# A banded attention with two MLPs on one core: low gates read last, four output banks, and tile 4 at the end of layer 1

## The chip, the core and the metric

The kernel runs on one core of one Trainium2 chip. The metric is the device time of one execution. Below, PE is TensorE (its weight loads are shown apart as PEld), DVE is VectorE, ACT is ScalarE, POOL is GpSimd, and SP is the engine that issues nearly all DMAs.

## The reference

Three stages follow each other; every sum has to come out in float32 quality.

```
attn  = softmax(q k^T / 8 + bias, causal, window 128) v      # 4 batches, 8 heads, 576 x 64
x     = attn, tokens by features                             # 2304 x 512
h     = x @ w_in  (512 x 2048);  g = max(0.01 h, h)          # layer 1
x     = g @ w_out (2048 x 512)
h     = x @ w2_in (512 x 2048);  g = h * sigmoid(1.702 h)    # layer 2
out   = g @ w2_out (2048 x 512)                              # 2304 x 512
```

## The kernel before, in words

**Numbers in two halves.** A float32 operand of a matmul is kept as a high part (what the fast matmul format holds) and a low part (the rest). A product is three matmuls: high times high, high times low, low times high. `PASS` (line 505) lists them as (weight part, gate or token part). A gate `g` is made in `split` (line 526): ACT copies the high part, then POOL subtracts it from the gate to get the low part, so the low part is ready last.

**Layer 1.** 2304 tokens stand in five tiles (`TW`: 384, 512, 512, 512 and 384 columns), the 2048 hidden features in 8 chunks of two blocks of 128. A round is one chunk and one tile: `mm1` twice (12 matmuls each, one block of hidden features), then one round later `mm2` four times (6 matmuls each, one block of 128 outputs). An evacuation on DVE adds each `mm2` result to the accumulator `y`. The table `rounds` (line 716) sets the order: chunks 0 and 1 interleaved while attention still runs, then chunk by chunk, tile 0 to 4. Two sets of weight tiles alternate: even chunks in `wA`, odd chunks in `wB`. Beside this, in the same loop, the float64 weights of both layers are converted to high and low parts on ACT, DVE and POOL, and those of layer 2 are stored to DRAM (`w7d`, `wod`).

**Layer 2** multiplies with seven products in place of eight (a Strassen scheme). The tokens form three pairs p of two blocks of 384 (pair 0: tiles 0 and 1; pair 1: tiles 2 and 3; pair 2: the rest with tile 4). `build_x` (line 576) makes seven operands of a pair from `y`: 7 copies on ACT, 11 subtractions on DVE, spread over steps. It starts with pair 0 near the end of layer 1, and pair 1 starts 16 steps later. The operands lie where layer 1's tokens were (`xblocks`), so each waits until layer 1 has read its tokens. A unit (chunk i, pair p) is the seven products `prod` (line 652) and then six `out2` (line 680), each 6 matmuls of 512 columns for 128 tokens. Chunk 0 interleaves pair 0 with the last `mm2` of layer 1; pair 1 follows. Chunks 1 to 6 run the 14 products of both pairs and then a tail of 12 `out2` (in chunk 6 six of these stand beside the next unit). Chunk 7 and all of pair 2 interleave products with the `out2` of the unit before.

**Weights of layer 2** go into 15 slots (`slots`, `old`), which are the last weight tiles of layer 1: slots 0 to 6 for the seven products, 7 to 10 and 11 to 14 for the output weights of even and odd chunks. Before, slots 0 to 6 and 7 to 10 lie in tiles of chunk 6 and of chunk 7's first layer, and the first loads are issued as soon as chunk 6 is through.

**PSUM.** Each tag has two banks. `mm2` takes "mm" and "O" in turn, `out2` only "mm". A product takes "S", "O" or "pt". The order on each engine is the order in which the code issues (a manual schedule); every engine works in that order.

Of the kernel before, what the change touches and what calls it, by code (L numbers as in the profile page):

```python
# [20 lines left out]
NTT = len(TW)  # L21
NF = DFF // 128
CB = 2
NCH = NF // CB
# [9 lines left out]
def attention_mlp_kernel(  # L34
# [16 lines left out]
    def ps(tag):  # L51
        return psum.tile([128, 512], F32, tag=tag, name=tag, bufs=2)
# [4 lines left out]
    step = [0]  # L57

    def after(d, fn):
        later.setdefault(step[0] + d, []).append(fn)  # L60
# [84 lines left out]
    pending = [0]  # L145
# [381 lines left out]
    def split(u, key, more):  # L527
# [4 lines left out]
        nc.scalar.activation(g[:, 0], u, AF.Copy)  # L532
        sub(nc.gpsimd, g[:, 1], u, g[:, 0].bitcast(F32))

    def mm2(r, e):
        _, c, t = r
        ops = [(f, a, b2) for f in range(CB) for a, b2 in PASS]
        assert all((c * CB + f, 1) in ready for f in range(CB))
        y = ps("mm" if window[0] else ("mm", "O")[e % 2])[:, 0:TW[t]]
        for m, (f, a, b2) in enumerate(ops):  # L540
            nc.tensor.matmul(  # L541
                out=y, lhsT=wt[c * CB + f][:, 2 + a, e * 128:(e + 1) * 128],
                rhs=gt[r, f][:, b2, :], start=(m == 0), stop=(m == len(ops) - 1),
            )
        acc = y1[t][:, e]

        def evac():
            if c == 0:
                nc.scalar.activation(acc, y, AF.Copy)
            else:  # L550
                nc.vector.tensor_tensor(out=acc, in0=acc, in1=y, op=ALU.add)  # L551

        after(1, evac)
# [6 lines left out]
    def xblocks(extra):  # L560
        halves = [extra[:, k].rearrange("p (a k) n -> p a k n", a=2) for k in range(2)]
        parts = xs.rearrange("p (m a k n) -> p m a k n", a=2, k=2, n=TT)
        parts = [parts[:, m] for m in range(2 * NT // TT)]
        halves = parts[0:4] + halves + parts[4:]
        for p in range(3):
            xb[p] = halves[7 * (p % 2):7 * (p % 2) + 7]

    def token_block(p, t, e):
        j = 2 * p + t
# [38 lines left out]
    def load_in(i, n):  # L608
        nc.sync.dma_start(
            out=slots[n].bitcast(F32), in_=w7d[i % NCH][:, n].rearrange("p a k -> p (a k)"))  # L610
# [68 lines left out]

    def out2(i, p, t, e):  # L680
        c = i % NCH
        y = ps("mm")
        ops = [(f, a, b2) for f in range(CB) for a, b2 in PASS]
        for m, (f, a, b2) in enumerate(ops):
            nc.tensor.matmul(  # L685
                out=y, lhsT=gt[i, p, f, t][:, b2, e * 128:(e + 1) * 128],
                rhs=out_slot(i, f, a), start=(m == 0), stop=(m == len(ops) - 1),
            )
        tile_, off = token_block(p, t, e)
        acc = y1[tile_][:, :, off:off + 128]  # L690

        def evac():
            yv = y.rearrange("p (e n) -> p e n", e=4)
            if c == 0:
                nc.scalar.activation(acc, yv, AF.Copy)
            else:
                nc.vector.tensor_tensor(out=acc, in0=acc, in1=yv, op=ALU.add)  # L697
            if c == NCH - 1:
                after(1, store)

        def store():
            for u in range(2):
                b, m = divmod((T0[tile_] + off) // 64 + u, NKB)
                t1 = b * S + 64 * ORDER[b % 2][m]

                (nc.scalar if u and i == 2 * NCH - 1 else nc.sync).dma_start(
                    out=out[t1:t1 + 64, :].rearrange("r (e n) -> r e n", e=4),
                    in_=acc[64 * u:64 * u + 64])

        after(1, evac)  # L710
# [3 lines left out]

    early = ((0,), (1,), (2,), (3, 4))
    rounds = [(0, c, t) for ts in early for c in range(2) for t in ts]
    rounds += [(0, c, t) for c in range(2, NCH) for t in range(NTT)]
    groups = []
    NR = len(rounds)

# [8 lines left out]
            groups += [(j - 1, mm2, e) for e in range(4)]  # L729
    groups.reverse()  # L730

    last1 = {c: j for j, (_, c, _) in enumerate(rounds)}
    pos1, pos2 = [-1], [-1]

# [17 lines left out]
    def layer1():  # L752
        raws[0] = 3
        q1 = wconv[4 * CB:]
        q2 = [(NF + f, 1) for f in range(CB)] + [(n, 0) for n in range(NF, 2 * NF)]
        todo, wait = [], 0
        while pos2[0] < NR - 4 or q1 or q2 or todo or pending[0]:


            while q1 or q2:  # L760
                near = q1 and slot_free(*q1[0], ahead=1)
                if len(wraw) >= (3 if near or not q2 else 2):
                    break
                todo.append(((q1 if near or not q2 else q2).pop(0), step[0]))
                load_w(*todo[-1][0])
            if todo and wait <= 0 and step[0] - todo[0][1] >= 4:
                n, p = todo[0][0]
                if n >= NF or slot_free(n, p):
                    todo.pop(0)
                    if n < NF:  # L770
                        if n not in wt:
                            alloc_w(n)
                        conv_w(n, p)
                    else:
                        (conv_out if p else conv_in)(n)
                    wait = 4
            if groups:
                run_group()
            tick()
            wait -= 1  # L780

    def layer2():
        raws[0] = 2
        xblocks(tmp([128, 2, 4, TT], F32R, "xe", 1))
        old = [wt[NF - 4 + n][:, m] for n in range(4) for m in range(4)]
        slots.extend(old[n] for n in (0, 1, 2, 3, 4, 5, 6, 8, 9, 12, 13, 10, 11, 14, 15))
        for n in USE:
            load_in(0, n)


        begun = None
        while len(groups) > 6:
            run_group()
            tick()
            if begun is None and pos2[0] >= NR - 4:
                begun = step[0]
                build_x(0, 1.6)
        assert begun is not None
        after(max(1, begun + 16 - step[0]), lambda: build_x(1, 1.3))
        prev = [run_group] * len(groups)  # L800

        def outs(i, p, t):
            return [lambda e=e: out2(i, p, t, e) for e in range(3)]

        def play(ops, at):
            for t, fn in enumerate(ops):
                for g in at.get(t, ()):
                    g()
                if fn is not None:
                    fn()  # L810
                elif prev:
                    prev.pop(0)()
                tick()

        def raw_out(n):
            return lambda: load_w(n, 1)

        def make_out(n):
            return lambda: conv_out(n)

        n0 = NF + CB
        for p in range(2):
            w = unit_ops(0, p)
            play([w[0], None, w[1], w[4], None, w[5], None, w[3], None, w[6], None, w[2], None],
                 {4: [raw_out(n0 + 1)], 1: [make_out(n0)]} if p else {6: [raw_out(n0)]})
            if not p:
                load_out(0)
            prev = outs(0, p, 1) + outs(0, p, 0)


        for i in range(1, NCH - 1):
            n0 = NF + CB * (i + 1)
            lead = [None] * (len(prev) if i == 1 else 0)
            w = [unit_ops(i, p) for p in range(2)]
            ops = lead + [w[p][n] for p, n in (
                (0, 0), (1, 0), (0, 5), (0, 4), (1, 4), (1, 5), (0, 3), (1, 3), (0, 1), (0, 6),
                (1, 6), (1, 1), (0, 2), (1, 2))]
            tail = [fn for t in (1, 0) for p in range(2) for fn in outs(i, p, t)]
            last = i == NCH - 2
            m = len(ops)  # L840
            at = {m - 10: [raw_out(n0)], m - 6: [raw_out(n0 + 1)], m: [make_out(n0)],
                  m + 5: [make_out(n0 + 1)]}
            if i == 1:
                at[1] = [make_out(NF + CB + 1)]
            play(ops + (tail[:6] if last else tail), at)
            if last:
                prev = tail[6:]


        for i, p in [(NCH - 1, 0), (NCH - 1, 1)] + [(NCH + c, 2) for c in range(NCH)]:  # L850
            w = unit_ops(i, p)
            play([w[0], w[5], w[1], w[4], None, None, w[3], None, None, w[6], w[2], None, None], {})
            if p and i < 2 * NCH - 1:
                load_out(i + 1)
            if (i, p) == (NCH - 1, 0):
                after(1, lambda: build_x(2, 1.6))
            prev = outs(i, p, 1) + outs(i, p, 0)
        for _ in range(4):
            tick()
        for fn in prev:  # L860
            fn()
            tick()
        while later:
            tick()
# [145 lines left out]
```

## Time and profile before

| | |
|---|---|
| Time, median of 3 runs | 898.65 us (898.63 to 899.36) |
| The profiled execution | 898.58 us, span 896.9 us |
| PE busy | 868.3 us, 97% of the span |
| DVE, ACT, POOL busy | 597.3, 422.4, 400.6 us |
| Mean granted clock of PE | 0.988 |

PE is busy in nearly all of the span. Attention and the first layer-1 rounds fill it to some 155 us, layer 1 to about 515 us, layer 2 the rest. Times of single instructions and groups stand in the rows below. What a stall of PE costs is read best from start to start of its matmul groups, since the end of a matmul is modelled.

### The profile page before, as it was taken

What the parts mean: (1) busy time and instruction counts of PE and PEld (TensorE: products, weight loads), DVE (VectorE), ACT (ScalarE), POOL (GpSimd) and SP (SyncE); (2) the same over time, 40 slices, a digit from 0 to 9 for tenths busy, and PEclk for the clock granted to TensorE, in tenths of its full rate; (3) what the DMA queues carried; (4) which work ended last, traced back from release to release, by engine and by line L of the source; (5) the groups of instructions that cost most, each with busy time, mean ns of one, the idle gap of its engine ahead of it and who ended that gap; (6) DMA issues with size and microseconds to landing.
All of it is one profiled execution on the core that took longest, in us unless ns stands there. A gap on an engine that the chain in (4) does not pass through costs nothing.

```text
span 896.9 us, 15695 instructions
## 1 busy us (share of the span) xinstructions
PE 868.3 (97%) x5722; PEld 759.0 (85%) x5722; DVE 597.3 (67%) x1213; ACT 422.4 (47%) x1025; POOL 400.6 (45%) x441
## 2 busy tenths in 40 slices
PE   7689999999999999999999989999999999999997
PEld 5578888889898988888898979889888988899896
DVE  5889765368799998998943753674574477323333
ACT  5887885453344433543333566245235435443331
POOL 5887544254466757565552133244144242232321
PEclk6999999999999999999999999999999999999999
DMA  9764430242244254425250144244324515956552
GB/s 219 175 168 114 102 87 13 84 141 71 71 156 146 97 176 145 162 94 189 70 188 1 48 129 144 73 137 153 117 84 153 157 67 152 304 168 208 165 177 71
DMA packets 85532, 116.04 MB, mean 129 GB/s; under 512 B 40912, under 2 KB 51152, under 8 KB 84432
## 3 DMA queue, kind: packets, MB, share of 16 engines
q1 hardware_dynamic: 82064, 113.83, 41.3%
q10 hardware_dynamic: 3392, 1.21, 0.5%
q8 instruction: 46, 0.75, 0.3%
q14 instruction: 30, 0.25, 0.1%
HBM read 87.23 MB, written 27.79 MB: 128 GB/s over the span
## 4 chain that ended last, share of the span: by engine, by line
PE 80%; DVE 8%; POOL 3%; issue 3%; DMA 3%; ACT 2%; SPq 0%; POOLq 0%; ACTq 0%; DVEq 0%
PE mm L685 21%; PE S L623 10%; PE mm L541 9%; PE pt L517 7%; PE O L541 7%; PE S L517 7%; PE pt L623 5%; PE O L623 3%; PE mm L517 2%; PE O L477 2%; PE pt L442 2%; PE S L393 2%; DVE ca L169 1%; DVE x L143 1%; DVE ca L167 1%
## 5 line engine op out<-in xcount | busy, mean ns | idle before, releaser
L143 POOL TENSOR_TENSOR g<-u,g 128x512 fp32r<-128x512 f32 (+1 forms) x86 | 112.7, 1314 | 124.2 <-ACT g L532 101.4
L175 POOL TENSOR_TENSOR ca<-ca,cb 128x512 f32<-128x512 f32 x59 | 81.5, 1381 | 114.6 <-DVE cb L173 102.6
L697 DVE TENSOR_TENSOR y<-y,mm 128x512 f32<-128x512 f32 x126 | 86.4, 685 | 53.7 <-PE mm L685 52.6
L685 PE MATMUL mm<-wB,g 128*128 128x512 f32 x432 | 118.4, 395 | 0.5 <-POOL g L143 0.5
L685 PE MATMUL mm<-wB,gm 128*128 128x512 f32 x432 | 118.4, 395 | 0.2
L143 POOL TENSOR_TENSOR g<-sn,g 128x384 fp32r<-128x384 f32 x42 | 43.4, 1039 | 132.5 <-ACT g L532 108.9
L685 PEld LDWEIGHTS mm<-wB,gm 128*128 128x128 f32 x432 | 79.4, 188 | 21.2 <-POOL gm L143 2.4
L685 PEld LDWEIGHTS mm<-wB,g 128*128 128x128 f32 x432 | 81.2, 189 | 17.4 <-POOL g L143 0.8
L623 PE MATMUL S<-x,wA 128*128 128x384 f32 x384 | 75.9, 336 | 2.3 <-ACT x L588 1.8
L649 DVE TENSOR_TENSOR sn<-sn,pt 128x384 f32<-128x384 f32 x48 | 26.6, 554 | 77.2 <-ACT sn L644 52.8
L644 ACT ACTIVATE sn<-S 128x384 f32<-128x384 f32 x72 | 35.3, 490 | 83.3 <-PE S L623 83.2
L623 PEld LDWEIGHTS S<-x,wA 128*128 128x128 f32 x384 | 67.8, 188 | 5.0 <-ACT x L588 2.1
L551 DVE TENSOR_TENSOR y<-y,mm 128x512 f32<-128x512 f32 (+1 forms) x74 | 46.2, 625 | 37.0 <-PE mm L541 36.9
L541 PE MATMUL mm<-g,wA 128*128 128x512 f32 (+1 forms) x264 | 62.9, 372 | 3.3 <-POOL g L143 2.4
L541 PE MATMUL mm<-g,wB 128*128 128x512 f32 (+1 forms) x264 | 62.2, 371 | 0.0
L143 POOL TENSOR_TENSOR gm<-sn,gm 128x384 fp32r<-128x384 f32 x30 | 32.2, 1080 | 65.4 <-ACT gm L532 51.0
L523 ACT ACTIVATE u<-S 128x512 f32<-128x512 f32 (+1 forms) x34 | 18.8, 552 | 85.4 <-PE S L517 85.4
L623 PE MATMUL pt<-x,wA 128*128 128x384 f32 x288 | 57.6, 337 | 0.5 <-DVE x L143 0.5
L541 PEld LDWEIGHTS mm<-g,wA 128*128 128x128 f32 x264 | 47.6, 188 | 10.2 <-POOL g L143 3.2
L169 DVE SCALAR_TENSOR_TENSOR ca<-raw,ca 128x512 uint32<-128x512 uint32 x62 | 55.5, 895 | 0.6
L167 DVE TENSOR_SCALAR ca<-ca 128x512 uint32<-128x512 uint32 x62 | 55.2, 891 | 0.5
L635 ACT ACTIVATE sn<-sn 128x384 f32<-128x384 f32 x72 | 37.3, 518 | 36.9 <-DVE sn L649 36.9
(131 smaller groups left out, 1878.1 us busy)
## 6 DMA issues: line engine op xcount, KB each, us to landing
wA<-w7d SPq DMA_DIRECT2D x112, 256.0 KB, 3.5
w7d<-c SPq DMA_DIRECT2D x8, 1792.0 KB, 7.0
wB<-wod SPq DMA_DIRECT2D x36, 256.0 KB, 4.0
raw<-w1i SPq DMA_DIRECT2D x16, 512.0 KB, 3.5
raw<-w1o SPq DMA_DIRECT2D x16, 512.0 KB, 3.7
raw<-w2o SPq DMA_DIRECT2D x16, 512.0 KB, 4.8
raw<-w2i SPq DMA_DIRECT2D x16, 512.0 KB, 3.5
wod<-wB SPq DMA_DIRECT2D x28, 256.0 KB, 2.8
```

The source lines that it names most:

```text
L143: e.tensor_tensor(out=out, in0=in0, in1=in1, op=ALU.subtract)
L167: lambda: nc.vector.tensor_scalar(a, a, 0x07FFFFFF, 3, op0=ALU.bitwise_and, op1=ALU.logical_shift_left),
L169: lambda: nc.vector.scalar_tensor_tensor(out=a, in0=hi32, scalar=0xC0000000, in1=a, op0=ALU.bitwise_and, op1=ALU.bitwise_or),
L175: lambda: nc.gpsimd.tensor_tensor(out=af, in0=af, in1=bf, op=ALU.add),
L517: nc.tensor.matmul(out=h, lhsT=w[:, a, k * 128:(k + 1) * 128], rhs=xt[t][:, b2, k], start=(m == 0), stop=(m == len(ops) - 1),)
L541: nc.tensor.matmul(out=y, lhsT=wt[c * CB + f][:, 2 + a, e * 128:(e + 1) * 128], rhs=gt[r, f][:, b2, :], start=(m == 0), stop=(m == len(ops ...
L551: nc.vector.tensor_tensor(out=acc, in0=acc, in1=y, op=ALU.add)
L623: nc.tensor.matmul(out=out, lhsT=w[:, 256 * a + 128 * k:256 * a + 128 * k + 128], rhs=x[:, b2, k], start=(start and m == 0), stop=(stop an ...
L635: nc.scalar.activation(u, h, AF.Gelu_apprx_sigmoid)
L644: nc.scalar.activation(st[name], st["X"], AF.Copy)
L685: nc.tensor.matmul(out=y, lhsT=gt[i, p, f, t][:, b2, e * 128:(e + 1) * 128], rhs=out_slot(i, f, a), start=(m == 0), stop=(m == len(ops) - 1),)
L697: nc.vector.tensor_tensor(out=acc, in0=acc, in1=yv, op=ALU.add)
```

## The change

There are five edits.

1. `gate_order` puts a group's matmuls on the low gate part last, in `mm2` and `out2`. In `out2` the gate block with index t comes first.
2. `out2` takes "mm" and "O" in turn for chunks 1 to 6.
3. In `rounds`, tile 4 of chunks 6 and 7 moves behind tiles 0 to 3 of both.
4. The first operand build starts one round earlier, at step 1.5 in place of 1.6. Pair 1's starts when tile 3 of chunk 7 is summed, at step 1.9 in place of 1.3. The operands of pair 1 that are built last are the ones on tile 4's memory.
5. Slots 2 to 6 and 7 to 10 lie on other weight tiles. The seven first loads no longer go out together: four go out after `mm1` of chunk 6's tile 4, two after that of chunk 7's, and one after `mm2` of chunk 6's.

```diff
+    def gate_order(fs):
+        return [(f, a, 0) for f in fs for a in range(2)] + [(f, 0, 1) for f in fs]
...
     def mm2(r, e):
-        ops = [(f, a, b2) for f in range(CB) for a, b2 in PASS]
+        ops = gate_order(range(CB))
...
+        xb[1] = [xb[1][n] for n in (0, 1, 4, 3, 5, 2, 6)]
...
     def out2(i, p, t, e):
-        y = ps("mm")
-        ops = [(f, a, b2) for f in range(CB) for a, b2 in PASS]
+        y = ps(("mm", "O")[e % 2] if 0 < i < NCH - 1 else "mm")
+        ops = gate_order((t, 1 - t))
...
-    rounds += [(0, c, t) for c in range(2, NCH) for t in range(NTT)]
+    rounds += [(0, c, t) for c in range(2, NCH - 2) for t in range(NTT)]
+    rounds += [(0, c, t) for ts in ((0, 1, 2, 3), (4,)) for c in (NCH - 2, NCH - 1) for t in ts]
...
-        while pos2[0] < NR - 4 or q1 or q2 or todo or pending[0]:
+        while pos2[0] < first or q1 or q2 or todo or pending[0]:
...
-        slots.extend(old[n] for n in (0, 1, 2, 3, 4, 5, 6, 8, 9, 12, 13, 10, 11, 14, 15))
-        for n in USE:
-            load_in(0, n)
+        slots.extend(old[n] for n in (0, 1, 2, 8, 4, 5, 9, 12, 13, 3, 6, 10, 11, 14, 15))
+        build_x(0, 1.5)
+        marks = [(0, last1[NCH - 2], (0, 1, 4, 5)), (0, last1[NCH - 1], (3, 6)),
+                 (1, last1[NCH - 2], (2,))]
...
-            if begun is None and pos2[0] >= NR - 4:
-                begun = step[0]
-                build_x(0, 1.6)
+            if not half_way and pos2[0] >= second:
+                half_way = True
+                build_x(1, 1.9)
+            while marks and (pos1, pos2)[marks[0][0]][0] >= marks[0][1]:
+                for n in marks.pop(0)[2]:
+                    load_in(0, n)
-        after(max(1, begun + 16 - step[0]), lambda: build_x(1, 1.3))
```

The first place is PE at the start of the tail of layer 2's chunk 1. The numbers tell buffers apart: `g_6167` and `gm_6185` are the two gates, and `mm` or `O` is the output bank. Before, three of its twelve output groups:

```order
L685 MATMUL mm_6226<-wB_169,gm_6185 128x512 x3
L685 MATMUL mm_6226<-wB_170,g_6167 128x512 x3
L685 MATMUL mm_6239<-wB_169,gm_6185 128x512 x3
L685 MATMUL mm_6239<-wB_170,g_6167 128x512 x3
L685 MATMUL mm_6251<-wB_169,gm_6185 128x512 x3
L685 MATMUL mm_6251<-wB_170,g_6167 128x512 x3
```

The same three groups in the changed kernel, on PE:

```order
L689 MATMUL mm_6226<-wB_170,g_6167 128x512 x2
L689 MATMUL mm_6226<-wB_169,gm_6185 128x512 x2
L689 MATMUL mm_6226<-wB_170,g_6167 128x512
L689 MATMUL mm_6226<-wB_169,gm_6185 128x512
L689 MATMUL O_6239<-wB_170,g_6167 128x512 x2
L689 MATMUL O_6239<-wB_169,gm_6185 128x512 x2
L689 MATMUL O_6239<-wB_170,g_6167 128x512
L689 MATMUL O_6239<-wB_169,gm_6185 128x512
L689 MATMUL mm_6251<-wB_170,g_6167 128x512 x2
L689 MATMUL mm_6251<-wB_169,gm_6185 128x512 x2
L689 MATMUL mm_6251<-wB_170,g_6167 128x512
L689 MATMUL mm_6251<-wB_169,gm_6185 128x512
```

The low part of `gm_6185` moves from the second matmul of the group to the sixth, and the middle one of three groups takes an "O" bank, so a bank of "mm" is used again three groups later and not two.

The second place is PE at the end of layer 1; `wA` are chunk 6's weights and `wB` chunk 7's, and L623 or L627 are products of layer 2. Before, from `mm2` of chunk 7's tile 2:

```order
L541 MATMUL mm<-g,wB 128x512 x6
L541 MATMUL O<-g,wB 128x512 x6
L541 MATMUL mm<-g,wB 128x512 x6
L541 MATMUL O<-g,wB 128x512 x6
L517 MATMUL S<-x,wB 128x384 x12
L517 MATMUL pt<-x,wB 128x384 x12
L541 MATMUL mm<-g,wB 128x512 x6
L541 MATMUL O<-g,wB 128x512 x6
L623 MATMUL S<-x,wA 128x384 x6
```

In the changed kernel, on PE, from the second half of the same `mm2`:

```order
L544 MATMUL mm<-g,wB 128x512 x6
L544 MATMUL O<-g,wB 128x512 x6
L517 MATMUL S<-x,wA 128x384 x12
L517 MATMUL pt<-x,wA 128x384 x12
L544 MATMUL mm<-g,wB 128x512 x6
L544 MATMUL O<-g,wB 128x512 x6
L544 MATMUL mm<-g,wB 128x512 x6
L544 MATMUL O<-g,wB 128x512 x6
L517 MATMUL S<-x,wB 128x384 x12
L517 MATMUL pt<-x,wB 128x384 x12
L544 MATMUL mm<-g,wA 128x384 x6
L544 MATMUL O<-g,wA 128x384 x6
```

The first product of layer 2 comes right behind these twelve rows. Between the end of chunk 7's tile 2 and that product there now stands a round more than before.

The third place is ACT in layer 2's pair 1 of chunk 0: `x<-y` is an operand copy of `build_x`, `sn<-S` reads a product's running sum, `wB<-ca` ends a weight conversion. Before:

```order
L588 ACTIVATE x<-y 128x768
L532 ACTIVATE gm<-sn 128x384
L644 ACTIVATE sn<-S 128x384
L164 ACTIVATE ca<-raw 128x512
L695 ACTIVATE y<-mm 128x4x128
L588 ACTIVATE x<-y 128x768 x2
L635 ACTIVATE sn<-sn 128x384
L644 ACTIVATE sn<-S 128x384
L588 ACTIVATE x<-y 128x768
L532 ACTIVATE gm<-sn 128x384
L695 ACTIVATE y<-mm 128x4x128 x2
L225 ACTIVATE wB<-ca 128x512
```

The same place on ACT in the changed kernel:

```order
L592 ACTIVATE x<-y 128x768
L639 ACTIVATE sn<-sn 128x384
L532 ACTIVATE gm<-sn 128x384
L648 ACTIVATE sn<-S 128x384
L164 ACTIVATE ca<-raw 128x512
L699 ACTIVATE y<-mm 128x4x128
L639 ACTIVATE sn<-sn 128x384
L648 ACTIVATE sn<-S 128x384
L532 ACTIVATE gm<-sn 128x384
L699 ACTIVATE y<-mm 128x4x128 x2
L225 ACTIVATE wB<-ca 128x512
```

Of the four copies that stood in this piece one is left at its head; the other three stand further ahead, beside pair 0.

## Rows read from the trace of the kernel before

**Rows 1.** Page, part 1: engine, busy us, share of the span, instructions.

```profile
PE 868.3 (97%) x5722; PEld 759.0 (85%) x5722; DVE 597.3 (67%) x1213; ACT 422.4 (47%) x1025; POOL 400.6 (45%) x441
```

**Rows 2.** Waits of the weight loads: us in total, times, longest.

```profile
PEld mm L685 <- POOL gm L143: 2.4, 6, 0.4
PEld S L623 <- ACT x L588: 2.1, 1, 2.1
PEld mm L685 <- DVE y L697: 1.9, 6, 0.5
```

**Rows 3.** Chain in order of time, undisturbed stretch: start us, us, what.

```profile
160.31 1.36 PE mm L541 x6
...
178.73 2.08 PE pt L517 x12
```

**Rows 4.** Timeline, tail of chunk 2: start, us, engine, what, [idle before].

```profile
590.11 1.98 POOL L143 TENSOR_TENSOR gm<-u,gm 128x384 fp32r<-128x384 f32 x2
...
590.74 1.16 PE L685 MATMUL mm<-wB,gm 128*128 128x512 f32 x3
...
591.17 0.30 PEld L685 LDWEIGHTS mm<-wB,gm 128*128 128x128 f32 x2 [0.41 <-POOL gm L143]
...
607.79 0.69 PE L623 MATMUL S<-x,wA 128*128 128x384 f32 x3
```

**Rows 5.** Timeline, pair 1 of chunk 0 in layer 2: PE, ACT and POOL.

```profile
515.06 0.53 ACT L532 ACTIVATE g<-u 128x384 fp32r<-128x384 f32 x1 [0.71 <-PE O L541]
515.73 1.44 POOL L143 TENSOR_TENSOR g<-u,g 128x384 fp32r<-128x384 f32 x1 [0.24 <-ACT g L532]
516.36 0.40 PE L685 MATMUL mm<-wB,g 128*128 128x512 f32 x1
517.22 1.43 PE L685 MATMUL mm<-wB,g 128*128 128x512 f32 x5 [0.47 <-POOL g L143]
518.49 1.22 PE L623 MATMUL O<-x,wA 128*128 128x384 f32 x6
519.56 0.65 ACT L164 ACTIVATE ca<-raw 128x512 f32<-128x512 f32 x1
521.48 0.62 PE L623 MATMUL S<-x,wA 128*128 128x384 f32 x2 [1.77 <-ACT x L588]
522.47 0.97 PE L623 MATMUL S<-x,wA 128*128 128x384 f32 x4 [0.38 <-DVE x L143]
523.28 2.59 PE L685 MATMUL mm<-wB,g 128*128 128x512 f32 x6
525.67 1.77 PE L623 MATMUL pt<-x,wA 128*128 128x384 f32 x6
527.29 1.55 PE L685 MATMUL mm<-wB,g 128*128 128x512 f32 x6
...
530.37 0.63 ACT L225 ACTIVATE wB<-ca 128x512 fp32r<-128x512 f32 x1 [0.89 <-POOL ca L175]
530.42 0.85 PE L685 MATMUL mm<-wB,gm 128*128 128x512 f32 x3
531.43 0.79 PE L623 MATMUL S<-x,wA 128*128 128x384 f32 x3 [0.16 <-ACT sn L644]
```

**Rows 6.** Page, part 5: line, engine, what, count | busy us, mean ns | idle before.

```profile
L175 POOL TENSOR_TENSOR ca<-ca,cb 128x512 f32<-128x512 f32 x59 | 81.5, 1381 | 114.6 <-DVE cb L173 102.6
...
L169 DVE SCALAR_TENSOR_TENSOR ca<-raw,ca 128x512 uint32<-128x512 uint32 x62 | 55.5, 895 | 0.6
L167 DVE TENSOR_SCALAR ca<-ca 128x512 uint32<-128x512 uint32 x62 | 55.2, 891 | 0.5
```

**Rows 7.** Windows: stretch; us; PE, PEld, DVE, ACT, POOL busy; PEclk; DMA; GB/s.

```profile
500.00:516.00 16.00, 16.00 (x88) 15.27 (x87) 14.10 (x19) 10.23 (x17) 3.04 (x4) 1.00 0.07 23
523.30:526.50 3.20, 3.20 (x10) 2.65 (x9) 3.17 (x5) 1.76 (x4) 0.00 (x0) 0.53 0.59 203
```

**Rows 8.** Loads of the product slots (line 609), issue to landing.

```profile
DMA to landing us min/median/max: 2.5/3.5/7.2
```

More of the change, by code (lines that the diff above doesn't have):

```diff
@@ L730, in attention_mlp_kernel @@
     groups.reverse()
+    first, second = (rounds.index((0, NCH - 1, t)) for t in (1, 3))
     last1 = {c: j for j, (_, c, _) in enumerate(rounds)}
@@ L785, in layer2 @@
         old = [wt[NF - 4 + n][:, m] for n in range(4) for m in range(4)]
-        slots.extend(old[n] for n in (0, 1, 2, 3, 4, 5, 6, 8, 9, 12, 13, 10, 11, 14, 15))
-        for n in USE:
-            load_in(0, n)
-        begun = None
+        slots.extend(old[n] for n in (0, 1, 2, 8, 4, 5, 9, 12, 13, 3, 6, 10, 11, 14, 15))
+        build_x(0, 1.5)
+        marks = [(0, last1[NCH - 2], (0, 1, 4, 5)), (0, last1[NCH - 1], (3, 6)),
+                 (1, last1[NCH - 2], (2,))]
+        half_way = False
         while len(groups) > 6:
@@ L794, in layer2, with first_run @@
             tick()
-            if begun is None and pos2[0] >= NR - 4:
-                begun = step[0]
-                build_x(0, 1.6)
-        assert begun is not None
-        after(max(1, begun + 16 - step[0]), lambda: build_x(1, 1.3))
-        prev = [run_group] * len(groups)
+            if not half_way and pos2[0] >= second:
[4 more added lines that the diff above has]
+                    load_in(0, n)
+        assert half_way
+        def first_run():
+            run_group()
+            while marks and (pos1, pos2)[marks[0][0]][0] >= marks[0][1]:
+                for n in marks.pop(0)[2]:
+                    load_in(0, n)
+        prev = [first_run] * len(groups)
         def outs(i, p, t):
```

## Prediction

> **What bounds the kernel now.** The page's table of engines comes first: PE is busy 868.3 of 896.9 us [rows 1], so a gain can only be time in which PE stood or ran slowly. The second view is the list of waits, and there the weight loads' queue rather than PE's own, since it shows what held a matmul back before the modelled end of the last one hides it. After attention three kinds of wait stand out: output matmuls on POOL's low gates (2.4 us, six times), the same line on DVE's evacuation (1.9 us, six times), and products of layer 2 on operand copies (2.1 us, once) [rows 2]. Such a wait runs beside matmuls still in flight, so the third view prices it: the chain gives PE's undisturbed pitch, 1.36 us for six matmuls of 512 columns (0.227 each) and 2.08 us for twelve of 384 (0.173 each) [rows 3]. What start-to-start times in the timeline have beyond that pitch is lost. The sum is made against the profiled execution, 898.6 us (the median of the runs is 898.65).
>
> **Tails of chunks 1 to 6 (edits 1 and 2).** In chunk 2, PE starts the tail at 590.74 and the next unit's first product at 607.79 [rows 4]: 17.05 us for 72 matmuls that need 72 x 0.227 = 16.32. Of the 0.73 us lost I put 0.13 to the change of size between products and outputs, which stays. The rest, 0.6, is two waits. The first is for a low gate: the second matmul reads it, POOL has two of them to make from 590.11 on, 0.99 us each, and the weight load goes through at 591.17, 0.41 us late [rows 4]. The new order reads that part sixth, at 590.74 + 5 x 0.227 = 591.88, which is 0.7 us after it was let through. The high part is read third now and was read first, so it gains room as well. The second wait is for a bank. With two banks, a group must find the evacuation done that came two groups before; with "O" for the middle one of three it is three groups, and one group is 1.36 us more room. The longest such wait is 0.5 us [rows 2]. Both kinds occur six times, once or so per tail, so the term is -6 x 0.6 = -3.6 us. The bounds are 0 and -6 x 0.73 = -4.4. What takes the waits' place is DVE, which also converts weights beside the tail; its backlog then shows as a late evacuation that PE reaches later, or not at all, because products of the next unit use other banks.
>
> **The seam between the layers (edits 3 to 5).** Pair 1's operands are late now. In rows 5, start to start against pitch: 516.36 to 517.22 loses 0.63, on to 518.49 another 0.14 (five matmuls), to 521.48 1.95 (1.04 needed), to 522.47 0.64 (0.35 needed), to 523.28 0.12. That is 3.5 us. Then the clock drops: after those idle stretches the window behind 523.30 shows a granted clock of 0.53, which is the lower level, 1.2 in place of 2.4 GHz, for nearly all of it [rows 7]. The six outputs from 523.28 take 2.39 in place of 1.36 us, the six of 384 columns from 525.67 take 1.62 in place of 1.04 [rows 5]: 1.6 us. Together 5.1.
>
> All of it should go, step by step. In the new order PE has 72 matmuls of 512 columns and 60 of 384 between chunk 7's tile 1 and the first product, 26.7 us (before 60 and 24, 17.8 us). Pair 0's operands are spread over 16 steps there. Pair 1's start four steps before the first product, in place of six behind it; their 20 steps end three steps after pair 1's first product, and by the order of DVE's queue each operand is whole some 6 us before its product. What hides them is the stretch of pair 0: 13 groups of 1.04 us. DVE is the engine to watch: it was already busy 14.1 of 16 us with pair 0's operands [rows 7], and in the new stretch pair 0's last and seven of pair 1's eleven subtractions meet seven evacuations and three sums. It is nearly full, so a lag of about a microsecond is possible; the 6 us cover that. If the cover failed, the loss would come back as before, up to 5.1.
>
> The first loss, 516.36 to 518.49, is a low gate again (POOL, 515.73 for 1.44 us [rows 5]). ACT could write that gate's high part only at 515.06, when the last `mm2` let go of the buffer, 0.26 us before pair 1's first product (516.36 - 1.04). The new order costs here: the buffer's low part is read two matmuls later, 0.35 us. So the high part starts 0.1 us after that product's start, plus 0.53 of ACT, 0.05 and 1.44 of POOL: ready at 2.1 us. It is read sixth, at 1.04 + 5 x 0.227 = 2.2 us. No wait, by a hair; bounds 0 and 0.6. A low part alone takes 0.99 [rows 4]; the 1.44 comes from DVE subtractions beside it, and I keep it. The Trainium skill (SBUF — State Buffer, section "SBUF: two separate sides") speaks against the change here: GpSimd and a DVE instruction with two SBUF inputs take their shared port pair as an exclusive lock, and the loser waits out the whole instruction. By that rule, estimated with a DVE instruction as long as POOL's own, the low part would take 1.98 us and PE would wait 0.5, which makes 891.0.
>
> **What is late next.** In pair 1 a product must not add to its bank before ACT has copied the running sum. At 531.43 that costs 0.44 (530.42 to 531.43 with 0.68 needed, and some 0.1 on the restart, as behind 517.22 [rows 5]), because ACT's copy stands behind the last conversion step, L225 at 530.37, which waits for POOL. The changed order keeps that queue. Now PE comes there sooner: from pair 1's first product on, five products (5 x 1.04) and four output groups (4 x 1.36) make 10.6 us. ACT reaches L164, where the conversion starts, after five instructions of 0.5 to 0.9 us, the first of them the gate of before: 3.1 us in. The conversion took from 519.56 to 531.00, 11.4 us, with operand work between its steps. Its own steps need 0.65 + 0.89 + 0.9 + 1.38 + 0.63 and three shorter ones, taken at 0.5: 6.0 [rows 5, 6]. With one operand subtraction, one sum and one gate subtraction left in its way, 0.5 to 0.9 each, I get 7.6 to 8.6, so the sum copy ends at 11.2 to 12.2 and PE waits 0.6 to 1.6. Bounds: nothing, if it needs 6.0, and 4.4 if it stays at 11.4. I take 1.0, so this place costs 0.6 more than before.
>
> **The loads.** Seven loads move behind the last reads of their tiles, and on SP everything queues behind them. Four leave when chunk 6's tile 4 has its `mm1`; until the first product PE has 5.4 + 4.2 + 2.1 = 11.7 us. Two leave after chunk 7's, 9.4 us before their product. One, and behind it a raw weight and the four output weights, leaves after the fourth `mm2` of chunk 6's tile 4, 6.2 us before its product and 9.4 before the outputs. Landing took 3.5 us in the middle and 7.2 at most [rows 8]. So I cost them at nothing; bounds 0 and 1.0 plus a clock drop of 1.6. The order of rounds as such costs nothing: same matmuls, same sizes. A weight part used twice in a row was no cheaper: `mm2` had such pairs and runs at that pitch all the same [rows 3]. In attention and in mid layer 1 a low gate is read a place later in two groups that wait; 0.1 us in all.
>
> Sum: 898.6 - 3.6 - 5.1 + 0.6 - 0.1 = 890.4 us, and I say 890.4.
>
> **Rivals.**
> A. *The seam keeps part of its wait.* DVE falls behind on two pairs' operands, or conversion stays slow before the sum copy. For it: DVE's 14.1 of 16 us, the queue behind L225. Against it: 6 us of room per operand, three of four copies gone from ACT's piece. It returns 2 to 5 us: 892.5 to 895.5, middle 893.8.
> B. *More banks don't help*, since DVE is the bound in the tails and evacuates late whatever the bank. For it: the waits end on DVE. Against it: they are short, and one group more is 1.36 us. It keeps half of the tail term: 892.2.
> C. *Slower: late loads.* The load for the last product of pair 0 leaves only 6.2 us ahead, with the output weights behind it. At 15 us, twice the slowest landing, PE would wait 8.8 us and drop its clock once, 1.6: 890.4 + 10.4 = 900.8. It decides from a landing of some 13 us. No row comes near that.
> D. *Better than the sum:* no wait before the sum copy and the whole 0.73 per tail gone: 890.4 - 1.0 - 0.8 = 888.6.
> That the edits don't do what they say is ruled out for the orders, which can be read; for the operands' start it is A.
>
> **How the numbers follow.** Forecast 0.56 (its own range 889.4 to 891.6), A 0.19, B 0.11, C 0.03, D 0.11. The range is 888.4 to 894.6: it takes in D, B and most of A. A change under 0.2% (1.8 us) can't be told from none here, so "no change" is 896.9 to 900.4; the far end of A and part of C give it 0.03. Slower 0.02, faster 0.95.
>
> **What would show it.** Right: no wait of output matmuls on POOL's `gm` or on DVE's `y` in the tails, 16.4 to 16.5 us from the tail's start to the next product, a granted clock of 1.00 through the seam, no wait of a product on an operand copy, and one wait on `sn` of 0.5 to 1.7 us in pair 1. Wrong: a wait of a product on a DMA, a clock near 0.5 anywhere after attention, or the six tails still at 17 us.

## The result and the profile after

The changed kernel takes 889.97 us in the median of four runs (888.95 to 892.39), the kernel before 898.64 beside it: a ratio of 0.991, interval 0.9886 to 0.9933. Five more rounds gave 889.60 (888.37 to 890.72) and 0.9905, interval 0.9890 to 0.9920. The profiled execution took 890.8 us, span 889.1. The forecast was 890.4.

Part 1 of the page and one row of part 5, to be held against [rows 1, 6]: PE is busy 6.8 us less, and the weight conversion's POOL step takes what it took.

```profile
PE 861.5 (97%) x5722; PEld 759.4 (85%) x5722; DVE 592.7 (67%) x1213; ACT 421.8 (47%) x1025; POOL 406.1 (46%) x441
...
L175 POOL TENSOR_TENSOR ca<-ca,cb 128x512 f32<-128x512 f32 x59 | 80.9, 1371 | 108.2 <-DVE cb L173 77.2
```

Waits of the weight loads from 500 us to the end, changed kernel. The three groups of [rows 2] are gone. What is left stood in the kernel before as well: the first row, on `g`, a gate of chunk 0 and not of the tails, has grown (its row before stands below), and the second, an operand of pair 2, is the same.

```profile
PEld mm L689 <- POOL g L143: 1.5, 1, 1.5
PEld pt L627 <- DVE x L143: 0.8, 1, 0.8
```

Before, the wait on `g`:

```profile
PEld mm L685 <- POOL g L143: 0.8, 1, 0.8
```

The tail of chunk 2 in the timeline, the answer to [rows 4]. From 586.48 to the next product at 602.84 are 16.36 us, where the pitch of [rows 3] asks for 16.32. POOL has the first of two `gm` done at some 586.85, half of 2.01 us after 585.84; the sixth matmul reads it at 587.63, and no wait stands on any row. The second group takes an "O" bank.

```profile
585.84 2.01 POOL L143 TENSOR_TENSOR gm<-u,gm 128x384 fp32r<-128x384 f32 x2
...
586.48 0.63 PE L689 MATMUL mm<-wA,g 128*128 128x512 f32 x2
586.94 0.62 PE L689 MATMUL mm<-wB,gm 128*128 128x512 f32 x2
...
587.63 0.40 PE L689 MATMUL mm<-wB,gm 128*128 128x512 f32 x1
587.87 0.62 PE L689 MATMUL O<-wA,g 128*128 128x512 f32 x2
...
602.84 2.27 PE L627 MATMUL S<-x,wA 128*128 128x384 f32 x12
```

The seam, pair 1 of chunk 0, for [rows 5]:

```profile
514.30 0.84 ACT L592 ACTIVATE x<-y 128x768 fp32r<-128x768 f32 x1
...
515.04 0.51 ACT L532 ACTIVATE g<-sn 128x384 fp32r<-128x384 f32 x1
...
515.65 0.95 DVE L143 TENSOR_TENSOR y<-y 128x768 f32<-128x768 f32 x1
515.68 1.80 POOL L143 TENSOR_TENSOR g<-sn,g 128x384 fp32r<-128x384 f32 x1 [5.73 <-issue]
515.79 1.20 PE L627 MATMUL S<-x,wA 128*128 128x384 f32 x6
515.87 0.53 ACT L532 ACTIVATE g<-u 128x384 fp32r<-128x384 f32 x1 [0.32 <-PE O L544]
...
516.98 1.32 DVE L143 TENSOR_TENSOR x<-y,x 128x768 fp32r<-128x768 f32 x1
...
517.45 1.71 POOL L143 TENSOR_TENSOR g<-u,g 128x384 fp32r<-128x384 f32 x1
...
517.76 0.40 PE L689 MATMUL mm<-wA,g 128*128 128x512 f32 x1
...
518.73 0.65 ACT L164 ACTIVATE ca<-raw 128x512 f32<-128x512 f32 x1
...
519.21 0.51 PE L689 MATMUL mm<-wB,g 128*128 128x512 f32 x1 [1.05 <-POOL g L143]
519.55 1.23 PE L627 MATMUL O<-x,wA 128*128 128x384 f32 x6
...
526.17 0.62 ACT L225 ACTIVATE wB<-ca 128x512 fp32r<-128x512 f32 x1
526.72 0.49 ACT L648 ACTIVATE sn<-S 128x384 f32<-128x384 f32 x1
...
527.91 0.86 PE L627 MATMUL S<-x,wB 128*128 128x384 f32 x4
```

No product of the seam waits for an operand. The first output group waits instead: 517.76 to 519.21 is 1.45 us for one matmul of 0.227, 1.22 lost, and 0.12 more before the product at 519.55: 1.34 together. POOL's low part of that gate came at 519.16, since POOL had two in a row: ACT had that gate's high part ready at 516.40 (515.87 + 0.53), and POOL turned to the low part only at 517.45. Last, the product at 527.91 starts after the sum copy (526.72 + 0.49) and doesn't wait.

The clock is whole, where [rows 7] had 0.53:

```profile
500.00:516.00 16.00, 16.00 (x95) 16.00 (x94) 12.32 (x19) 9.43 (x17) 4.59 (x4) 1.00 0.39 126
523.30:526.50 3.20, 3.20 (x18) 2.94 (x17) 0.57 (x1) 1.44 (x4) 2.48 (x2) 1.00 0.97 302
```

The slot loads, now line 613, landed as in [rows 8] or sooner:

```profile
DMA to landing us min/median/max: 2.6/3.3/5.9
```

The output weights queued behind them took longer, as the DMA view of 507 to 512 us shows (count, size, median us to landing):

```profile
wB<-wod SPq DMA_DIRECT2D x2, 256.0 KB, 6.1
wA<-wod SPq DMA_DIRECT2D x2, 256.0 KB, 6.3
```

Where the time went, by the starts of the same matmuls in both traces. "Seam" is from pair 1's first product over 7 products and 6 output groups (pitch: 42 x 0.173 + 36 x 0.227 = 15.4 us); "tails" is from there to the first product behind the sixth tail.

| kernel | seam | tail of chunk 2 | tails | time |
|---|---|---|---|---|
| before | 21.08 | 17.05 | 189.80 | 898.58 profiled |
| changed | 16.99 | 16.36 | 185.69 | 890.80 profiled |
| changed, again | 16.96 | 16.36 | 185.69 | 889.71 profiled |
| e1_two_banks | 16.98 | 16.52 | 186.61 | 890.6, one run |
| e2_old_out_order | 17.88 | 16.67 | 187.45 | 892.3, one run |
| e3_no_seam | 21.10 | 16.36 | 185.69 | 893.53, 4 runs |
| e4_seam_alone | 19.48 | 17.06 | 189.71 | 896.25, 10 runs |
| e5_pace2 | 17.63 | 16.36 | 185.69 | 888.6, one run |
| e6_pace2_conv | 16.60 | 16.36 | 185.69 | 888.8, one run |
| e7_pair2 | 16.60 | 16.36 | 185.69 | 888.43, 5 runs |
| e8_two_raws | 16.97 | 16.36 | 185.69 | 889.9, one run |
| e9_last_copy | 15.64 | 16.36 | 185.69 | 886.77, 4 runs |

The changed kernel gains 4.09 us in the seam and 4.11 in the tails, and loses 0.47 up to pair 1's first product. That loss is the start's: its attention waited 4.2 us on the DMA `y<-v` and the kernel before's 2.1, and by 114 us it was 0.61 behind. The second profile of the changed kernel was 0.37 ahead there, and 0.59 at pair 1's first product. Single times differ by some microseconds (the changed kernel's ten lie between 888.37 and 892.39), so the table's pieces are compared, not the single times.

### The profile page after: what moved, and what is told of

It is laid out like the page before. It is cut to its first block, busy times and chain, and to the rows that moved or that the text cites. A ratio compares the mean times of both kernels' runs of the same rounds, so it can differ in the third digit from the quotient of the medians.

```text
span 889.1 us, 15665 instructions
## 1 busy us (share of the span) xinstructions
PE 861.5 (97%) x5722; PEld 759.4 (85%) x5722; DVE 592.7 (67%) x1213; ACT 421.8 (47%) x1025; POOL 406.1 (46%) x441
## 3 DMA queue, kind: packets, MB, share of 16 engines
q10 hardware_dynamic: 3392, 1.21, 0.5%
## 4 chain that ended last, share of the span: by engine, by line
PE 81%; DVE 6%; DMA 4%; issue 3%; POOL 3%; SPq 1%; ACT 1%; ACTq 0%; POOLq 0%
PE mm L689 18%; PE S L627 11%; PE mm L544 10%; PE pt L517 8%; PE O L544 7%; PE S L517 7%; PE pt L627 5%; PE O L689 4%; PE O L627 3%; PE mm L517 2%; PE O L477 2%; PE pt L442 2%; PE S L393 2%; DMA y<-v 1%; DVE ca L169 1%
## 5 line engine op out<-in xcount | busy, mean ns | idle before, releaser
L143 POOL TENSOR_TENSOR g<-sn,g 128x384 fp32r<-128x384 f32 x42 | 46.9, 1123 | 129.5 <-ACT g L532 93.0
L701 DVE TENSOR_TENSOR y<-y,mm 128x512 f32<-128x512 f32 x102 | 70.0, 687 | 47.1 <-PE mm L689 45.9
L689 PE MATMUL mm<-wB,gm 128*128 128x512 f32 x288 | 87.2, 391 | 0.0
L689 PE MATMUL mm<-wB,g 128*128 128x512 f32 x252 | 82.7, 392 | 1.1 <-POOL g L143 1.1
L648 ACT ACTIVATE sn<-S 128x384 f32<-128x384 f32 x72 | 35.3, 491 | 83.4 <-PE S L627 83.2
L689 PEld LDWEIGHTS mm<-wB,gm 128*128 128x128 f32 x288 | 53.9, 188 | 10.8
L627 PE MATMUL pt<-x,wA 128*128 128x384 f32 x288 | 57.0, 334 | 0.5 <-DVE x L143 0.5
L689 PEld LDWEIGHTS mm<-wB,g 128*128 128x128 f32 x252 | 47.1, 188 | 10.7 <-POOL g L143 1.5
L627 PE MATMUL S<-x,wA 128*128 128x384 f32 x288 | 56.1, 336 | 0.0
L436 POOL TENSOR_SCALAR st<-st,sm 128x192 f32<-128x192 f32 (+2 forms) x100 | 43.8, 459 | 25.5 <-PE pt L442 8.4
L169 DVE SCALAR_TENSOR_TENSOR ca<-raw,ca 128x512 uint32<-128x512 uint32 x62 | 53.0, 855 | 0.6
L544 PEld LDWEIGHTS mm<-g,wB 128*128 128x128 f32 x264 | 47.8, 188 | 5.8
```

The source lines that it names most:

```text
L143: e.tensor_tensor(out=out, in0=in0, in1=in1, op=ALU.subtract)
L169: lambda: nc.vector.scalar_tensor_tensor(out=a, in0=hi32, scalar=0xC0000000, in1=a, op0=ALU.bitwise_and, op1=ALU.bitwise_or),
L436: nc.gpsimd.tensor_scalar(w, w, sm[s][:, 3, m:m + 1], 1.0, op0=ALU.mult, op1=ALU.mult)
L544: nc.tensor.matmul(out=y, lhsT=wt[c * CB + f][:, 2 + a, e * 128:(e + 1) * 128], rhs=gt[r, f][:, b2, :], start=(m == 0), stop=(m == len(ops ...
L627: nc.tensor.matmul(out=out, lhsT=w[:, 256 * a + 128 * k:256 * a + 128 * k + 128], rhs=x[:, b2, k], start=(start and m == 0), stop=(stop an ...
L648: nc.scalar.activation(st[name], st["X"], AF.Copy)
```

## The experiments

**e1_two_banks.** The changed kernel with `out2` on one tag.

```diff
-        y = ps(("mm", "O")[e % 2] if 0 < i < NCH - 1 else "mm")
+        y = ps("mm")
```

> The changed kernel with out2 on the two banks of "mm" again (edit 2 undone); the low gates stay last. A full tail (first output matmul of chunks 1 to 5 to the next unit's first product) took 17.05 us in the kernel before and 16.36 in the changed one, 16.32 being PE's pitch. Theory (both edits are needed, each pays for its own wait): the gate wait of some 0.31 stays away and the bank waits of some 0.28 come back, so 16.65 us per tail and six tails 1.7 us longer than in the changed kernel. Rival (order alone does it; DVE's backlog came from the stall): 16.36. Second rival (DVE is the bound, so banks only moved the wait): also 16.36, with a late evacuation elsewhere.

Measured: 16.52 in chunk 2 and 186.61 over the tails, 0.92 more than with four banks. The wait that came back is the bank's:

```profile
PEld mm L689 <- DVE y L701: 1.4, 5, 0.3
```

So banks are worth 0.15 us a tail beside the new order, less than the 0.3 expected and not nothing.

**e2_old_out_order.** Four banks, but `out2` in the old order.

```diff
-        ops = gate_order((t, 1 - t))
+        ops = [(f, a, b2) for f in range(CB) for a, b2 in PASS]
```

> The changed kernel with the old order of matmuls in out2 alone (low gates second and fifth, block 0 first); four banks and the new order in mm2 stay. Theory: PE waits again for the low gate at the second matmul of each tail, about 0.31 with its restart, so 16.67 us per full tail; no bank waits. Rival (banks alone do it): 16.36. In pair 1 of chunk 0 the low gate is read second, so the wait there grows from 1.34 to about 2.2 us, and the clock may fall behind it.

Measured: 16.67 in chunk 2, as expected, and 187.45 over the tails. All six waits on `gm` are back, and pair 1's wait in the seam is 2.15 us in place of 1.22. The clock stayed at 1.00.

```profile
PEld mm L689 <- POOL gm L143: 2.4, 6, 0.4
```

Alone the banks gain 189.80 - 187.45 = 2.35 us and the order 189.80 - 186.61 = 3.19, both 4.11, so 1.4 us is gained by either. That is, in the main, the bank wait of a tail's fourth group. In the old order the second evacuation of a tail comes late, 4.37 us after the tail's start in chunk 2 as against 3.65 in the new order, because DVE's conversion step in front of it (L167) takes twice as long. It does so with two banks and with four; with four no matmul needs that bank yet. Here are the kernel before and e1_two_banks in chunk 2; why the order of PE's matmuls changes L167 wasn't tested.

```profile
593.23 1.28 DVE L167 TENSOR_SCALAR ca<-ca 128x512 uint32<-128x512 uint32 x1
...
587.68 0.62 DVE L167 TENSOR_SCALAR ca<-ca 128x512 uint32<-128x512 uint32 x1
```

The bank wait that e1_two_banks keeps stands at the tenth group (in one tail the eighth).

**e3_no_seam.** The kernel before with edits 1 and 2 alone.

> The kernel before with edits 1 and 2 alone (low gates last, four banks); rounds, slots, loads and operand builds as before. Theory (tails and seam are independent): tails as in the changed kernel, 16.36 us each, worth 4.1; the seam keeps its loss of some 5, since an earlier PE only waits longer for the late operands of pair 1. Time 894.5 us, clock down again in the seam. Rival (the low-gate wait at the seam's start is saved as well): 893.8.

Measured: 893.53 us (892.77 to 894.28), ratio 0.9942, interval 0.9926 to 0.9958. The two times expected differ by less than starts do, so the pieces decide: the tails gain the whole 4.11, the seam nothing. The 0.75 us that PE lost on the low gate at the seam's start are gone, but the product behind then lost 2.70 us on ACT's copy in place of 1.94, and the wait on the running sum 0.93 in place of 0.43. So the seam's 21.10 holds the product's wait on ACT's copy and a clock of 0.66 behind it, as the window from 520 to 524 shows.

```profile
520.00:524.00 4.00, 2.67 (x7) 2.17 (x8) 3.12 (x6) 2.53 (x5) 0.21 (x1) 0.66 0.17 56
```

**e4_seam_alone.** Edits 3 to 5 alone: `mm2` and `out2` as before.

> The changed kernel with edits 1 and 2 undone, so that only the seam is new. Theory: no wait on operands and no such wait before the sum copy; but the low gate of pair 0's last gate comes 3.4 us behind pair 1's first product and is read second, at 1.3, so PE waits 2.1 there. If the clock holds, the seam gains 3.2 and the time is 895.4; if it falls as it did before, 897.0. The tails stay at 17.05. Rival (the seam's gain does not depend on the order): 894.5.

Measured: 896.25 us (893.31 to 898.70), ratio 0.9972, interval 0.9957 to 0.9988. In the profiled execution its seam of 19.48 is 2.5 us longer than the changed kernel's: 0.9 are the longer wait on POOL's gate (2.15), as in e2_old_out_order, and 1.6 the clock, 0.51 behind that wait.

```profile
520.00:523.00 3.00, 3.00 (x11) 3.00 (x11) 2.14 (x6) 0.60 (x2) 0.00 (x0) 0.51 0.20 46
```

**e10_old_order_again and e11_seam_again.** The same wait of 2.15 us had cost the clock in e4_seam_alone and not in e2_old_out_order, so both ran once more.

> The kernel of e2_old_out_order once more. In e2_old_out_order PE stood 2.15 us in pair 1's first output group and the granted clock stayed at 1.00; in e4_seam_alone it stood the same 2.15 us and the clock then showed 0.51 over 520 to 523, which cost 1.5 us. Theory: which of the two happens differs from execution to execution, so here the stall is again 2.1 to 2.2 us and the clock may fall or not; if it falls, the seam takes 19.4 us in place of 17.9. Rival: it is the kernel's (what PE did before the stall), and then the clock stays at 1.00 again and the seam at 17.9.

> The kernel of e4_seam_alone once more. Theory: as in e10_old_order_again, the fall of the clock behind the 2.15 us stall differs from execution to execution; the spread of this kernel's ten times, 893.3 to 898.7, would fit that, and the seam then takes 17.9 or 19.5 us. Rival: it is the kernel's, and the clock falls again to about a half over 520 to 523, with a seam of 19.5.

Measured: the wait is 2.15 us in both, seams 17.91 and 17.89, clock 1.00 in both. Here is e11_seam_again in the stretch where e4_seam_alone, the same kernel, had 0.51:

```profile
520.00:523.00 3.00, 3.00 (x18) 2.83 (x17) 2.83 (x6) 1.93 (x4) 0.00 (x0) 1.00 0.30 61
```

It is the execution's, not the kernel's, and the 1.6 us is a risk that a 2 us stall carries: one of the four executions paid it.

**e5_pace2.** What makes pair 1's first gate late? A wider spread of pair 1's operand build puts one operand copy on ACT behind the gates in place of between them. (Other copies, and DVE's subtractions, move a place or two with it.)

```diff
-                build_x(1, 1.9)
+                build_x(1, 2.0)
```

> The changed kernel with pair 1's operand build spread at 2.0 in place of 1.9; on ACT one operand copy (0.84 us) then stands behind pair 0's last two gates and not between them, the order on PE and POOL is the same. Theory (POOL's queue): the 1.34 us that PE loses in pair 1's first output group comes from two low gates in a row on POOL, 1.80 and 1.71 us, the first of them started late, at 515.68, because that copy held up the gate's high part on ACT. Without it POOL starts some 0.6 us sooner, so the group loses 0 to 0.7 us. In exchange the wait of the running sum behind L225, which the late PE had covered, shows with 0.2 to 0.8 us some 11 us later. From the first product of pair 1 to the first tail the kernel gains 0.3 to 0.9 us on the changed kernel. Rival (the second gate alone decides): its high part starts at the same time, when mm2 lets go of its buffer, and its low part takes 1.7 to 1.8 us beside DVE whatever stands ahead of it; the group still loses 1.2 to 1.4 us and no wait on the running sum appears.

Measured: the wait on POOL is gone altogether (the output group from 513.96 runs into the product at 515.35 without a gap). Two waits on `sn` are there in its place, 0.84 and 0.90 us, so the seam is 0.64 longer, not shorter. The timeline, all engines:

```profile
511.09 1.01 POOL L143 TENSOR_TENSOR g<-sn,g 128x384 fp32r<-128x384 f32 x1 [4.00 <-issue]
...
513.67 1.02 POOL L143 TENSOR_TENSOR g<-u,g 128x384 fp32r<-128x384 f32 x1 [1.57 <-ACT g L532]
513.77 1.74 DVE L143 TENSOR_TENSOR y<-y 128x768 f32<-128x768 f32 x1
...
515.54 0.85 ACT L592 ACTIVATE x<-y 128x768 fp32r<-128x768 f32 x1 [0.87 <-DVE y L143]
516.29 0.51 ACT L532 ACTIVATE gm<-sn 128x384 fp32r<-128x384 f32 x1
516.70 0.47 ACT L648 ACTIVATE sn<-S 128x384 f32<-128x384 f32 x1
...
517.23 0.98 PE L627 MATMUL S<-x,wA 128*128 128x384 f32 x4 [0.67 <-ACT sn L648]
...
524.49 0.63 ACT L225 ACTIVATE wB<-ca 128x512 fp32r<-128x512 f32 x1 [1.47 <-POOL ca L175]
525.03 0.47 ACT L648 ACTIVATE sn<-S 128x384 f32<-128x384 f32 x1
...
525.55 1.32 PE L627 MATMUL S<-x,wB 128*128 128x384 f32 x6 [0.73 <-ACT sn L648]
```

Theory and rival differ by whether POOL's start decides, and it does: the first low gate now ran 2.6 us ahead of the second (511.09, 513.67) and both took 1.0. So the queue in front of the second gate and the length of each subtraction went together here; the rows of the changed kernel tell them apart, as the next section does. The rows name the two new waits as well: the sum copy (L648) at 516.70 stands behind an operand copy that itself waited for DVE, and the one at 525.03 behind L225.

**e6_pace2_conv.** e5_pace2, with the conversion one step later, which puts L225 behind the sum copy.

```diff
-                 {4: [raw_out(n0 + 1)], 1: [make_out(n0)]} if p else {6: [raw_out(n0)]})
+                 {4: [raw_out(n0 + 1)], 2: [make_out(n0)]} if p else {6: [raw_out(n0)]})
```

> The kernel of e5_pace2 with the weight conversion of pair 1 started one step later, which puts its last step on ACT, L225, behind the copy of the running sum that PE waits for. Theory: if the 0.2 to 0.8 us wait on sn in e5_pace2 is L225's doing, it is gone here, and the seam is 0.9 to 1.3 us shorter than in the changed kernel. Rival: the sum is late for another reason (DVE's sums), then the wait on sn stays, or the weights that are converted later become the new wait.

Measured: 16.60. The wait behind L225 is gone, so it was that; the first one stays, so only 0.4 us is left of the 0.9 to 1.3.

```profile
518.49 1.32 PE L627 MATMUL S<-x,wA 128*128 128x384 f32 x6 [0.67 <-ACT sn L648]
```

**e7_pair2.** e6_pace2_conv with pair 2's operands built closer.

```diff
-                after(1, lambda: build_x(2, 1.6))
+                after(1, lambda: build_x(2, 1.4))
```

> The kernel of e6_pace2_conv with pair 2's operand build spread at 1.4 in place of 1.6, so that it ends sooner. Theory: the one stall that both the kernel before and the changed one show at the start of pair 2 (a product waits for DVE's operand, PE loses 0.75 us near 751.8) goes, and with what e6_pace2_conv gains the kernel is 1.0 to 2.1 us faster than the changed one, 0.12 to 0.23%. Rival: closer operand work delays DVE's evacuations or ACT's gates beside it, PE waits there instead, and nothing is gained beyond e6_pace2_conv.

Measured: 888.43 us (887.29 to 889.76), ratio 0.9893, interval 0.9879 to 0.9908. Pair 2's wait is gone. This is the place in the changed kernel, a product held up after two of its six matmuls:

```profile
751.80 0.97 PE L627 MATMUL pt<-x,wA 128*128 128x384 f32 x4 [0.47 <-DVE x L143]
```

And the same product in e7_pair2, in one piece:

```profile
749.30 1.20 PE L627 MATMUL pt<-x,wA 128*128 128x384 f32 x6
750.34 1.20 PE L627 MATMUL O<-x,wA 128*128 128x384 f32 x6
```

By the starts that is 0.76 us, so with the seam's 0.4 the gain on the changed kernel is 1.1. **after_again**, the changed kernel in the same rounds, is the second profile of the table.

> The changed kernel once more, timed in the same rounds as e7_pair2. Theory: ratio 0.991 again (0.989 to 0.993), its seam with one loss of 1.2 to 1.4 us in pair 1's first output group, clock 1.00 there. Rival: the loss on POOL's gates there differs from execution to execution, as its place beside DVE does, and this profile shows 0.5 us less or more.

The loss in pair 1's first group was 1.23 us again: not a matter of the execution.

**e8_two_raws.** How near are late loads? One more 512 KB load goes out ahead of the output weights.

```diff
-                 {4: [raw_out(n0 + 1)], 1: [make_out(n0)]} if p else {6: [raw_out(n0)]})
+                 {1: [make_out(n0)]} if p else {6: [raw_out(n0), raw_out(n0 + 1)]})
```

> The changed kernel with the second raw weight load (512 KB) moved on SP from behind pair 1's first slot loads to ahead of the four output-weight loads, nothing else. It tests how near late loads (rival C of the prediction) are. In the changed kernel the first three output weights landed at 514.89, 515.49 and 516.13, 0.7 to 0.9 us before their matmuls at 516.83 and 517.06. If the queue is limited by what it moves, 512 KB more (one raw load took 3.6 us to land) put the output weights 1.2 to 1.8 us later: an output matmul of pair 1's first group waits on a DMA for 0.3 to 1.0 us, but the wait on POOL's gate at the end of that group, 1.2 us, hides most of it, so the seam is within 0.4 us of the changed kernel's 17.0. If the queue has bandwidth to spare, the landings move by less than 0.7 us and no matmul waits on a DMA.

Measured (DMA view of 506 to 511 us): the output weights land 7.0 and 7.4 us after issue, and they were issued later too. Counted from pair 1's first product, the last two land 1.6 us later than in the changed kernel, within the 1.2 to 1.8 expected, and PE loses 0.40 and 0.32 us on them. The wait on POOL shrinks by nearly as much, to 0.40, and the seam stays at 16.97.

```profile
wB<-wod SPq DMA_DIRECT2D x2, 256.0 KB, 7.0
wA<-wod SPq DMA_DIRECT2D x2, 256.0 KB, 7.4
```

PE in the timeline of the same kernel:

```profile
516.39 1.04 PE L689 MATMUL mm<-wA,g 128*128 128x512 f32 x2 [0.24 <-DMA wA<-wod]
...
518.37 0.50 PE L689 MATMUL mm<-wB,g 128*128 128x512 f32 x1 [0.23 <-POOL g L143]
```

**e9_last_copy.** e7_pair2 with pair 1's last operand copy one place later in the build's list, which at this spread puts it two steps later and behind the sum copy.

```diff
-(9, diff(b21, b22, b21)), (9, hi(6, b21)),
+(9, diff(b21, b22, b21)), (10 if p == 1 else 9, hi(6, b21)),
```

> The kernel of e7_pair2 with the last operand copy of pair 1 (0.85 us on ACT, for the product that is read last) one step later, so that it stands behind the copy of the running sum and not before it. Theory: the 0.84 us wait of a product on sn that e5_pace2, e6_pace2_conv and e7_pair2 show is that copy in ACT's queue; it goes, the seam from pair 1's first product to the first tail takes 15.7 to 15.9 us (after: 17.0, e7: 16.6), and the kernel is 0.7 to 0.9 us faster than e7_pair2, some 2.0 us (0.22%) faster than the changed kernel. Rival: the sum is late for DVE's or PE's sake, then the wait stays at 0.6 or more; or the operand is late now, then a wait on x appears at the last product of pair 1.

Measured: 886.77 us (886.45 to 886.97), ratio 0.9874, interval 0.9857 to 0.9890: the fastest of all. The seam takes 15.64, 0.2 over the bare pitch, and from 500 us on no matmul and no weight load waits. In the timeline the sum copy (L648) stands ahead of the operand copy (L592):

```profile
515.64 0.53 ACT L532 ACTIVATE gm<-sn 128x384 fp32r<-128x384 f32 x1
516.07 0.47 ACT L648 ACTIVATE sn<-S 128x384 f32<-128x384 f32 x1
...
517.54 0.84 ACT L592 ACTIVATE x<-y 128x768 fp32r<-128x768 f32 x1
```

By pieces it beats the changed kernel by 1.35 us in the seam and 0.76 at pair 2, 2.1 in all; the medians are 2.8 to 3.2 apart, and the rest is within what starts differ by.

## Why the prediction came out right, and where its steps failed

The time was right (890.4 forecast, 890.8 profiled), the direction too. Three of the terms were not (the tails, the low gate and the sum copy), and they nearly cancel. That the forecast came within half a microsecond is therefore in part luck. Both things that rival D asked for came true, no wait before the sum copy and nearly the whole loss of the tails gone; the low gate took back what D would have gained.

**Tails.** Forecast -3.6, measured -4.11, both waits gone as described. The mis-sized term is the 0.13 us "change of size between products and outputs, which stays": of it 0.04 stayed (16.36 against 16.32). Rival B is out by the changed kernel and e2_old_out_order: with four banks DVE's evacuations end no wait, in either order. It is the order, though, more than the banks, that brought the gain (3.19 alone as against 2.35).

**Seam, operands and clock.** Of the -5.1, the operands and the clock, 4.3, came in full: no product waits on an operand and the clock is 1.00. That DVE would keep up held (12.3 of 16 us busy up to 516, not more than the 14.1 of before). Rival A is out. The other 0.8 of the 5.1 is the low gate.

**Seam, the low gate.** This step failed: "No wait, by a hair; bounds 0 and 0.6" was 1.34 us. The working got ACT right (the high part was done at 516.40, as forecast) and let POOL be free then. It wasn't: the gate ahead had started only at 515.68, as ACT wrote its high part (515.04) behind an operand copy (514.30), and took 1.80. So the second started 1.0 us after it could have, and took 1.71 in place of 1.44: the queue is most of the loss. e5_pace2 moved that copy, among others, and the wait was gone. I had counted what is queued on ACT and DVE and not on POOL, the engine that ends the wait. By the lock that the Trainium skill states (SBUF — State Buffer, section "SBUF: two separate sides"), whichever starts first, a DVE instruction with two SBUF inputs or a GpSimd one that reads SBUF, keeps the port pair for its whole instruction. The traces agree: in the changed kernel DVE started first (515.65) and POOL took 1.80; in e5_pace2 POOL started first (513.67, 1.02) and DVE's subtraction, else 0.95, took 1.74. But the estimate by that rule gave 0.5 us of wait (890.9, where the prediction has 891.0), since it too had no queue in it.

**Seam, the sum copy.** Forecast: a wait of 1.0 where 0.44 had been; measured: none, so one of the prediction's own signs, the wait on `sn`, stayed away. The chain itself came as worked out, 8.06 us from L164 to the end of L225 (518.73 to 526.79; forecast 7.6 to 8.6), and the sum copy ended 11.4 us after pair 1's first product (forecast 11.2 to 12.2). But PE came 1.34 us late, by the step above, and so found it done; without that loss it would have reached the product at 526.57, 0.64 us before the copy's end at 527.21. In e5_pace2, where the gate's loss is gone, the wait is there with 0.90 us, though the chain also began later there. The two errors, +1.34 and -1.0, belong to one another: a stall ahead of a wait pays for it.

**Loads.** At no cost, as said, but the margin was misjudged. Rival C looked at pair 0's last product and put the turning point at a landing of 13 us; that load landed in 2.8. The thin place was the queue behind it: the last two output weights landed at 515.49 and 516.13, 1.3 and 0.9 us before the matmuls at 516.83 and 517.06 that read them (e8_two_raws's expectation pairs them otherwise), and e8_two_raws reached the turning point with one more load in front.

**The other 0.1.** It didn't come: the stall of mid layer 1 that DVE's sum ends stood in both kernels (0.95 us of PE after, 0.78 before). From start to start the low gate just ahead of it lost 0.23 us in place of 0.41, but the wait on DVE then lost 1.21 in place of 1.06. Between 114 and 374 us nothing moved.

In sum: seam 4.09 in place of 4.5, tails 4.11 in place of 3.6, 0.1 not found, and 0.47 lost ahead of pair 1, in the start.

## What to carry to other kernels

A wait is priced at the engine that ends it: list everything in that engine's queue, and the start of the instruction ahead, before one duration is put in a sum. When a stall is taken out, ask which wait behind it was paid for by that stall: in e3_no_seam the time saved at the low gate was lost at the next product, and e5_pace2 took out one stall and met two waits, which e6_pace2_conv and e9_last_copy ended one by one, by putting the copy that PE waits for ahead of other work in ACT's queue. Compare the starts of the same instruction in both traces rather than totals, since a noisy start hides a microsecond.

## What the hardware showed that was not expected

- The same 2.15 us wait of PE dropped the granted clock in one of four executions (0.51 over 3 us, 1.6 us lost) and left it at 1.00 in three; two of these four are one kernel, e4_seam_alone and e11_seam_again. In the kernel before, where PE stood for longer in several pieces, and in e3_no_seam, where it lost 2.70 us at once, it fell in the profiles shown.
- A POOL subtraction of 128x384 that met a DVE subtraction of 128x768 took 1.02 us when it began first, with DVE's going from 0.95 to 1.74. When DVE began first, POOL took 1.80. Two in a row on POOL, with DVE's next between them, took 1.80 and 1.71 and DVE's 1.32: the price was paid again for each.
